# State cleared by VectorE and a new written-out order for the early tasks of a retention and feed-forward kernel

## The chip, the cores and the metric

The kernel runs on one core of a Trainium2 chip. The metric is the device time in microseconds (us), the median of several runs. The profile is of one execution of the same program.

## The reference

The inputs q, k and v have 4 batches, 8 heads, 768 steps and a head dimension of 64. First comes a retention layer: per head a state decays by gamma and takes in an outer product at each step, and the output is the query times the state. Then, on the 512 columns of all heads together, come a layer norm and a feed-forward block with a residual.

```python
for t in range(S):
    state = gamma[None, :, None, None] * state + np.einsum('bhd,bhe->bhde', k[:, :, t], v[:, :, t])
    y[:, :, t] = scale * np.einsum('bhd,bhde->bhe', q[:, :, t], state)
# x: y as (B, S, H * D)
xn = (x - mu) / np.sqrt(var + 1e-06) * g_ln
ch = np.maximum(xn @ w_ch1, 0.0) @ w_ch2
return x + ch
```

The weights are 512 x 2048 and 2048 x 512.

## The kernel before

**Tiles.** The 4 x 768 rows are 24 tiles of 128 rows. Tiles 0 to 3 are the first chunk of each batch, tiles 4 to 8 the chunks 1 to 5 of batch 0, and so on. Within a tile the retention is computed as masked attention; between the chunks of a batch it goes through the state (`pb` in the planner, the tile `state` on the chip, two buffers).

**Loads.** GpSimd issues the loads of q, k and v (one tile each, L430) and of the weights (L438), which arrive converted to bf16. Each weight is loaded in four quarters, here w1_0 to w1_3 and w2_0 to w2_3. Only q and k of tile 0 come another way (L401). From tile 9 on a small copy into `scrap` (L447) makes a load wait until an earlier load has landed.

**The tasks of a tile t** below 8, with the names used further on:

- tk, tq: TensorE transposes k and q into PSUM (L498, L505). ek: ScalarE copies k out (`trk`, L256). eq: VectorE scales q out (`trq`, L510).
- pa: TensorE, scores (L538). am: VectorE masks them into `asb` (L562). py: TensorE, scores times v (L586), and from chunk 1 on the query times `state` (L582).
- bn, xn: VectorE, statistics and the normalised row tile (L601, L613). xc: ScalarE keeps a copy of the row (L619).
- tx: TensorE transposes xn (L672), ex: ScalarE copies it to `xnt` (L256). sq and rs give `rstd` (L694 on ScalarE, L700 on VectorE).
- vg: GpSimd scales v (L633); pd: TensorE adds k times vg to the running sum in PSUM (L645); pb: VectorE writes the diagonal blocks of `state` from it (L659). The other blocks of `state` stay zero, which is why both buffers are cleared once (`c_zero`, L341).
- m1(g, ho): TensorE, group g of rows times four 128-column blocks of the first weight (L719), which starts at block ho. In the first eight groups a group is one tile, so m1(g, 0) needs w1_0, m1(g, 4) needs w1_1, m1(g, 8) w1_2, m1(g, 12) w1_3. re: relu on ScalarE (L732) or VectorE (L734).
- m2: TensorE, the second weight (L757), which needs all of w2; VectorE adds the residual (L767) and ScalarE sends the result off (L774).

From tile 8 on the transposes of q and k are made by DMA (L520), issued from SyncE.

**What sets the order.** The tasks are numbered as they are added. The list `ORDER`, written out by hand, gives the sequence in which they are emitted: a number modulo 10000 is the task, the ten thousands choose the engine where two are possible, the hundred thousands one of two PSUM banks. Every engine runs its own tasks in that sequence. The class `Plan` goes through the list with a fixed cost for each task and each load and so has a planned start for each. These planned times serve one purpose: `fill` looks at TensorE's planned gaps before `FILL_END` (14 us) and before the first task that takes `pd`, and puts matmuls on a zero tile there (L785) for a share `FILL` of the gap. `w_pad` is the time that the planner adds to the landing of a weight quarter.

Of the kernel before, what the change touches and what calls it, by code (L numbers as in the profile page):

```python
# [14 lines left out]
PE, ACT, DVE, POOL, SP = range(5)  # L15
# [4 lines left out]
              "k3", "q3", "v3", "w1_2", "k4", "q4", "v4", "k5", "q5", "v5", "w1_3", "w2_0",  # L20
              "k6", "q6", "v6", "k7", "q7", "v7", "w2_1", "w2_2", "w2_3"],
    "bufs": {"qsb": 6, "ksb": 5, "vsb": 9, "qk": 8, "tr": 6, "vg": 3, "trq": 3, "trk": 3},
    "load_pad": 600, "w_pad": 1500, "lead": 32, "lead2": 32, "sq_at": 28000, "late_load": 1700, "two": 4, "m2b": ("b0",), "m2all": 16, "inter": 4, "every": 4, "tail": (0, 384, 512), "step": 8, "pace": 8, "ahead": 3,
    "slack": 600, "tr_pad": 4000, "x_pad": 3500, "vg_pad": 2500, "fill": 0.8, "fill_end": 14000,
}

ORDER = [int(x) for x in """
16 17 2 0 3 19 20 23 14 8 15 1 24 5 7 9 25 4 10 6 21 11 26 18 22 146 45 100147 149 148  # L30
27 150 28 151 153 46 162 100163 29 152 154 164 165 30 155 12 166 31 156 167 32 157 158
159 47 168 176 13 524 169 179 214 100177 170 525 33 215 178 171 172 216 180 34 173 181
532 35 526 36 533 182 37 190 527 534 183 193 38 100191 184 535 48 192 185 186 194 187
195 49 540 542 541 196 204 543 528 197 39 207 100205 198 536 529 40 200 42 43 41 206 544
50 217 234 52 51 53 10537 55 208 100224 54 199 201 545 550 209 225 548 551 210 227 44
226 251 202 549 552 228 218 56 211 546 553 547 222 275 212 219 538 229 235 220 100241
554 539 530 10555 221 213 242 244 531 243 230 231 556 560 57 174 557 258 561 245 261 236
232 233 558 100237 562 238 246 259 247 10559 260 566 563 564 567 262 252 570 203 248 249
254 565 188 255 568 60 250 569 263 100722 160 61 58 59 268 62 287 253 298 63 723 716 724
301 66 264 67 64 717 65 725 269 718 161 571 175 189 719 265 726 266 720 576 100271 270  # L40
276 307 267 578 272 579 577 239 728 273 68 69 278 277 72 729 730 731 318 73 279 70 299
71 280 580 572 732 281 300 282 74 322 284 223 286 734 735 75 288 581 283 285 736 302 303
290 289 573 737 291 738 574 319 584 292 740 741 293 320 294 296 742 308 304 240 585 78
575 743 582 744 295 297 310 333 79 76 309 77 339 586 305 583 311 80 746 587 334 747 312
335 313 314 274 316 323 81 256 315 748 84 350 749 351 588 592 317 325 85 82 83 379 750
589 257 324 354 326 727 602 86 752 87 753 327 328 329 603 593 590 754 755 594 591 330 90
331 340 352 332 342 756 341 343 721 380 598 321 599 595 91 758 336 759 344 760 761 596
733 88 345 89 355 762 346 368 348 353 600 92 757 745 739 337 597 347 93 764 96 349 97 94
381 601 95 765 98 338 357 604 356 766 606 386 99 605 382 607 767 358 306 359 383 614 612
768 360 384 615 361 613 363 770 397 102 771 103 100 362 772 398 365 364 763 369 101 104  # L50
371 370 773 403 610 372 608 774 611 373 776 616 609 399 366 105 374 387 108 109 617 375
618 414 367 377 106 107 777 620 418 751 376 378 389 619 110 388 778 390 779 622 415 391
385 404 780 392 393 621 623 630 782 395 111 114 429 115 631 394 112 400 456 113 433 626
116 624 117 396 406 120 121 416 405 430 783 627 625 407 784 431 408 628 419 409 634 785
410 629 632 411 412 457 118 119 122 413 421 635 786 445 633 420 123 788 126 458 422 127
789 646 124 423 424 790 425 427 647 401 125 426 428 791 642 638 434 436 792 435 794 795
796 639 643 465 769 437 438 640 417 439 440 442 128 797 459 641 129 441 446 443 476 132
644 798 432 402 133 645 636 130 448 447 648 131 134 138 637 460 650 449 450 649 800 651
461 451 452 801 802 477 454 803 444 775 480 462 453 466 478 455 135 491 804 136 137 468
492 467 806 139 495 807 469 470 140 493 808 471 141 809 472 142 474 473 475 652 653 654  # L60
481 483 482 484 810 655 656 658 143 510 479 485 144 787 506 805 657 799 145 659 660 661
486 662 507 496 487 489 664 663 488 508 490 666 498 497 665 499 667 668 670 669 500 671
501 502 672 673 504 511 812 674 503 505 676 513 512 675 514 678 463 677 680 515 679 682
813 681 814 683 516 494 811 509 517 781 519 464 518 520 815 100830 831 816 521 832 818
819 200824 820 825 684 817 793 685 826 690 688 691 827 689 694 696 833 695 522 686 697
687 708 709 821 698 699 692 693 523 822 848 700 828 834 702 100842 701 703 706 707 704
200836 714 837 705 715 712 838 849 843 713 710 711 850 844 845 839 846 851 840 100854
852 855 856 823 847 841 835 829 853 857 860 861 858 862 863 864 859 865
""".split()]


# [90 lines left out]
def kernel(  # L162
# [16 lines left out]
    nc = tc.nc  # L179
# [158 lines left out]

    def c_zero(eng):
        for x in state:  # L340
            nc.gpsimd.memset(x, 0.0)  # L341

    a = plan.add
    small = a(DVE, 1200, -100, c_small)
# [11 lines left out]
    qscd = a(ACT, 700, -91, c_qsc, [args, table])  # L356
    maskd = a(DVE, 1230, -50, c_mask, [vscd, tri])
    gchd = a(ACT, 900, 100, c_gch, [small, qscd, vscd], at=9000)
    zerod = a(POOL, 500, 0, c_zero, at=9000)
    exps = [gchd, qscd, vscd]  # L360

    def c_gb(eng):
# [101 lines left out]
    for g in range(NG):  # L464
        for ho in range(HO):
            unit["1", g, ho] = u
            u += GROUPS[g] / 4
            every = CFG["every"] if GROUPS[g] == 1 else 8 if 12 <= G0[g] < 16 and GROUPS[g] == 2 else 4
# [239 lines left out]
    for g in range(NG):  # L708
        n = GROUPS[g]
        hb, h0 = buf_of[g]  # L710
        two = GMAX // n
# [109 lines left out]
```

## Time and profile before

| | |
|---|---|
| time, median of 3 runs | 214.54 us (214.35 to 215.2) |
| span of the profiled execution | 213.4 us |
| TensorE busy | 203.9 us (96%) |
| VectorE, ScalarE, GpSimd busy | 119.8, 86.3, 96.4 us |
| granted TensorE clock | 1.000 |
| moved by DMA | 26.85 MB |
| GpSimd's two memsets of `state` | 1.11 us, from 12.40 us |
| filler matmuls (L785) | 24, from 1.18 to about 12 us |

The busy times overlap; an engine's share says how full it is and not what it costs. The chain that ended last consists of TensorE for 87%, DMA for 4%, GpSimd for 4% and ScalarE for 2%. In the lines of the profile a group shows its start or its busy time, the engine, the line of the code and what it writes and reads; brackets hold the idle time ahead of it and what ended that.

### The profile page before, as it was taken

The numbers are of one execution on the slowest core, as the hardware profiler recorded it, in microseconds if no ns is written. First come the engines' busy times: TensorE is split into PE (matmuls) and PEld (weight loads), VectorE is DVE, ScalarE is ACT, GpSimd is POOL, SyncE is SP. The second block draws the span as 40 slices with busy tenths as digits, with TensorE's granted clock in tenths as the row PEclk, the third lists the DMA queues.
The fourth block names the chain that finished last, engine by engine and source line by source line (L and its number), as shares of the span: only waits on it lengthen the run. The fifth ranks groups of instructions, "written<-read, shape, count | busy, mean of one in ns | idle before, by whom it ended". The sixth has DMA issues, their size and how long they took to land.

```text
span 213.4 us, 4941 instructions
## 1 busy us (share of the span) xinstructions
PE 203.9 (96%) x2005; PEld 130.6 (61%) x2027; DVE 119.8 (56%) x260; ACT 86.3 (40%) x175; POOL 96.4 (45%) x151
## 2 busy tenths in 40 slices
PE   7977999999999999999999999999999999999992
PEld 3457989985667666666676676574454444444452
DVE  4876666863665874663775777578676510030041
ACT  5465677660421333332352442351376601544200
POOL 8997797249577464667845947430000000000000
PEclk9999999999999999999999999999999999999999
DMA  9999999999999999999999999939440250000035
GB/s 128 177 179 180 164 195 177 207 133 121 128 98 100 111 125 158 177 269 154 128 112 198 96 184 102 159 76 147 100 151 1 84 164 3 0 0 0 0 145 202
DMA packets 108890, 26.85 MB, mean 126 GB/s; under 512 B 101569, under 2 KB 105921, under 8 KB 108866
## 3 DMA queue, kind: packets, MB, share of 16 engines
q0 software_dynamic: 77024, 13.37, 81.2%
q1 hardware_dynamic: 27186, 6.59, 21.0%
q10 hardware_dynamic: 4656, 6.56, 8.8%
q8 instruction: 16, 0.26, 0.5%
q14 instruction: 8, 0.07, 0.1%
HBM read 27.30 MB, written 6.29 MB: 157 GB/s over the span
## 4 chain that ended last, share of the span: by engine, by line
PE 87%; DMA 4%; POOL 4%; ACT 2%; issue 1%; DVE 0%; POOLq 0%
PE b L757 39%; PE mm L719 38%; DMA k<-in_k_dram 4%; PE pa L538 2%; PE pd L645 2%; PE b L572 2%; PE b L548 2%; POOL v L430 1%; POOL k L430 1%; POOL qsb L430 1%; POOL w L438 1%; PE b L498 1%; ACT L694 1%; PE b L672 1%; ACT h L732 1%
## 5 line engine op out<-in xcount | busy, mean ns | idle before, releaser
L719 PE MATMUL mm<-xnt,w 128*128 128x128 bf16 (+2 forms) x896 | 95.2, 257 | 1.0 <-ACT xnt L256 0.9
L757 PE MATMUL b<-w,h 128*128 128x512 bf16 (+2 forms) x379 | 88.4, 370 | 1.2 <-issue 0.2
L732 ACT ACTIVATE h<-mm 128x512 bf16<-128x512 f32 x93 | 55.0, 598 | 83.6 <-PE mm L719 80.5
L719 PEld LDWEIGHTS <-w 128*128 128x128 bf16 x896 | 66.1, 98 | 21.4 <-issue 1.1
L757 PEld LDWEIGHTS <-h 128*128 128x128 bf16 x400 | 37.0, 98 | 37.7
L562 DVE TENSOR_TENSOR asb<-pa,mask 128x1024 bf16<-128x1024 f32 x24 | 29.4, 1224 | 19.6 <-PE pa L538 19.2
L767 DVE SCALAR_TENSOR_TENSOR osb<-b,rstd,x_all 128x512 f32<-128x512 f32 (+2 forms) x25 | 18.0, 727 | 27.3 <-PE b L757 27.0
L601 DVE BATCH_NORM_STATS2 bns<-b 128x6 f32<-128x256 f32 (+1 forms) x40 | 17.8, 478 | 17.4 <-PE b L572 11.0
L619 ACT CAST x_all<-b 128x256 bf16<-128x256 f32 (+1 forms) x40 | 16.2, 417 | 22.6 <-DVE xn L613 20.1
L613 DVE SCALAR_TENSOR_TENSOR xn<-b,mv,gb 128x256 bf16<-128x256 f32 (+1 forms) x40 | 20.1, 533 | 0.8
L633 POOL TENSOR_TENSOR vg<-vsb,vsc 128x512 bf16<-128x512 bf16 x16 | 16.6, 1044 | 5.6 <-PE pd L645 5.3
L430 POOL DMA_DIRECT2D vsb<-in_v_dram x20 | 18.1, 906 | 1.7 <-issue 1.6
L659 DVE TENSOR_TENSOR state<-pd,gch 64x256 bf16<-64x256 f32 x40 | 16.6, 414 | 4.1 <-PE pd L645 3.2
L430 POOL DMA_DIRECT2D qk<-in_k_dram x16 | 14.3, 892 | 2.2 <-issue 2.2
L430 POOL DMA_DIRECT2D qk<-in_q_dram x16 | 14.2, 886 | 1.0 <-issue 1.0
L447 POOL COPY scrap<-vsb 1x1 bf16<-1x1 bf16 x15 | 2.6, 176 | 19.2 <-DMA vsb<-in_v_dram 19.2
L447 POOL COPY scrap<-qk 1x1 bf16<-1x1 bf16 x30 | 5.3, 176 | 13.0 <-DMA qk<-in_k_dram 11.1
L700 DVE RECIPROCAL rstd<-rstd 128x1 f32<-128x1 f32 (+2 forms) x14 | 2.0, 157 | 13.4 <-ACT rstd L694 13.4
L785 PE MATMUL pd<-zeros 128*128 128x512 bf16 (+1 forms) x24 | 6.6, 420 | 1.3 <-DVE zeros L291 1.2
L572 PEld LDWEIGHTS <-asb 128*128 128x128 bf16 x128 | 5.8, 98 | 2.4
L438 POOL DMA_DIRECT2D w<-in_moe_w_ch_dram x8 | 6.3, 787 | 2.1 <-DMA w<-in_moe_w_ch_dram 2.0
L430 POOL DMA_DIRECT2D qsb<-in_q_dram x7 | 6.4, 909 | 1.8 <-DMA k<-in_k_dram 1.3
(68 smaller groups left out, 127.7 us busy)
## 6 DMA issues: line engine op xcount, KB each, us to landing
out_dram<-osb ACTq DMA_DIRECT2D x23, 256.0 KB, 3.4
w<-in_moe_w_ch_dram POOLq DMA_DIRECT2D x8, 512.0 KB, 10.3
vsb<-in_v_dram POOLq DMA_DIRECT2D x20, 128.0 KB, 5.5
qk<-in_k_dram POOLq DMA_DIRECT2D x16, 128.0 KB, 5.0
qk<-in_q_dram POOLq DMA_DIRECT2D x16, 128.0 KB, 5.2
qsb<-in_q_dram POOLq DMA_DIRECT2D x7, 128.0 KB, 8.9
v<-in_v_dram POOLq DMA_DIRECT2D x4, 128.0 KB, 6.7
ksb<-in_k_dram POOLq DMA_DIRECT2D x4, 128.0 KB, 9.4
```

Of the source, the lines that this page charges most:

```text
L430: nc.gpsimd.dma_start(out=tile_of(kind, j), in_=src)
L562: nc.vector.tensor_tensor(out=take("asb", t, [P, NPAIR, 2, P], BF16).rearrange("p i a t -> p a i t"), in0=held["pa", t], in1=mask.rearrang ...
L572: nc.tensor.matmul(half_y[h % 2][:, h // 2 * D:(h // 2 + 1) * D], lhsT=held["asb", t][:, h // 2, h % 2, :], rhs=tile_of("v", t)[:, h, :], ...
L601: nc.vector.bn_stats(out=bns[:, t, i, :], in_=x)
L613: nc.vector.scalar_tensor_tensor(out=dst, in0=src, scalar=mv[:, t, 0:1], in1=g, op0=ALU.subtract, op1=ALU.mult)
L619: nc.scalar.copy(out=dst, in_=src)
L633: e.tensor_tensor(out=take("vg", j, [P, H, D], BF16), in0=tile_of("v", j), in1=vsc[:, cc, :].unsqueeze(2).to_broadcast([P, H, D]), op=ALU. ...
L659: nc.vector.tensor_tensor(out=held["pb", n][o, :, o], in0=held["pd", b][o, :, o], in1=gch[o, cc, :].unsqueeze(2).to_broadcast([D, NPAIR, D ...
L719: nc.tensor.matmul(p[:, j, :], lhsT=w1[:, ko, (ho + j) * P:(ho + j + 1) * P], rhs=held["xnt", hb][:, h0:h0 + n, ko, :], start=(ko == 0), s ...
L732: nc.scalar.activation(out=dst, in_=src, func=AF.Relu)
L757: nc.tensor.matmul(held[key][:, 0:w], lhsT=held["h1", hb][:, ho, i * P:(i + 1) * P], rhs=w2[:, ho, cols], start=(ho == 0), stop=(ho == HO ...
L767: nc.vector.scalar_tensor_tensor(out=take("osb", key, [P, w], FP32), in0=held[key][:, 0:w], scalar=rstd[:, t:t + 1], in1=x_all[:, t, cols] ...
```

## The change

VectorE clears the two buffers of the state, in the stretch where the constants are made, instead of GpSimd between the loads. The list `ORDER` has a new first part, searched with landing times of the loads that were measured; the first 291 of its 866 entries are rearranged, and the rest is as it was. `w_pad` goes from 1500 to 550. No arithmetic changes.

```diff
-    "load_pad": 600, "w_pad": 1500, "lead": 32, "lead2": 32, "sq_at": 28000, "late_load": 1700, "two": 4, "m2b": ("b0",), "m2all": 16, "inter": 4, "every": 4, "tail": (0, 384, 512), "step": 8, "pace": 8, "ahead": 3,
+    "load_pad": 600, "w_pad": 550, "lead": 32, "lead2": 32, "sq_at": 28000, "late_load": 1700, "two": 4, "m2b": ("b0",), "m2all": 16, "inter": 4, "every": 4, "tail": (0, 384, 512), "step": 8, "pace": 8, "ahead": 3,
...
-16 17 2 0 3 19 20 23 14 8 15 1 24 5 7 9 25 4 10 6 21 11 26 18 22 146 45 100147 149 148
-27 150 28 151 153 46 162 100163 29 152 154 164 165 30 155 12 166 31 156 167 32 157 158
+16 17 2 0 3 19 20 23 14 8 15 1 24 5 7 9 25 4 10 6 13 21 11 26 18 45 22 27 44 28 146 46
+100147 149 148 150 151 29 30 31 32 47 162 152 165 214 33 100163 153 164 154 155 166 156
...
     def c_zero(eng):
         for x in state:
-            nc.gpsimd.memset(x, 0.0)
+            nc.vector.memset(x, 0.0)
...
-    zerod = a(POOL, 500, 0, c_zero, at=9000)
+    zerod = a(DVE, 480, -94, c_zero)
```

Read by engine, the list's new part is as follows. TensorE, tasks 11 to 64 (the first ten and all from the 65th on are the same):

```text
before: tk2 m1(0,0) tq2 pd0 tx1 pa2 m1(1,0) m1(0,4) py2 tk3 m1(1,4) tq3 tx2 pa3 m1(2,0)
        m1(2,4) py3 tk4 m1(0,8) tq4 m1(1,8) tx3 m1(2,8) pa4 | tk5 m1(3,4) tq5 m1(3,0) py4
        m1(3,8) pa5 pd4 m1(2,12) m1(1,12) pd5 tx4 tk6 m1(3,12) m1(0,12) tq6 py5 m1(4,0)
        m1(4,8) tk7 pa6 m1(4,4) tx5 m1(4,12) tq7 py6 m1(5,4) m1(5,0) pa7 pd6
after:  tk2 tq2 m1(0,0) pa2 pd0 tx1 m1(0,4) py2 m1(1,4) tk3 m1(1,0) tq3 tx2 pa3 m1(2,0)
        m1(1,8) py3 tk4 m1(2,8) tq4 m1(0,8) tx3 m1(2,4) pa4 | tk5 pd4 tq5 m1(3,0) m1(3,4)
        py4 pd5 m1(3,12) m1(3,8) pa5 tx4 m1(2,12) m1(0,12) py5 m1(1,12) tk6 m1(4,0) tq6
        m1(4,4) tx5 m1(4,8) pa6 tk7 tq7 m1(4,12) m1(5,4) py6 m1(5,0) pd6 pa7
```

GpSimd, where a name is a load and `clear` the memsets:

```text
before: v0 k1 q1 v1 w1_0 k2 q2 w1_1 v2 k3 q3 v3 w1_2 clear vg0 k4 q4 v4 k5 q5 v5 w1_3 w2_0
        k6 q6 k7 q7 v6 w2_1 vg4 vg5 w2_3 w2_2 k8 v8 q8 v7 vg6 ...
after:  v0 k1 q1 v1 w1_0 k2 v7 q2 w1_1 v2 k3 q3 v3 w1_2 vg0 k4 q4 v4 k5 q5 v5 w1_3 vg4 w2_0
        k6 vg5 q6 q7 w2_3 w2_1 k7 v6 w2_2 v8 k8 vg6 q8 ...
```

ScalarE has the first square root, with the load of its table, right after ex of tile 0; before, the first one stood after ek of tile 5 (the table load at 29.83 us). VectorE gets the clearing ahead of the cast of q0, and five relus of this part in place of three.

## The prediction

> **What bounds the kernel now.** I read the busy slices of the page first, then the list of what TensorE waited for, then the timelines of TensorE and of GpSimd, and last the single DMA issues with their times to landing.
>
> ```profile
> PE   7977999999999999999999999999999999999992
> DMA  9999999999999999999999999939440250000035
> ```
>
> From the fifth slice (about 21 us) on, TensorE is 90% busy or more until the last slice. The DMA engines are busy from the second slice on. By GpSimd's timeline the loads are a continuous stream until about 48 us, and from there each waits for an earlier one. So the end is set by TensorE's amount of work plus whatever TensorE loses, and what it loses lies early. The list of TensorE's waits sizes the loss:
>
> ```profile
> PE pd L785 <- DVE zeros L291: 1.2, 1, 1.2
> PE mm L719 <- ACT xnt L256: 0.9, 2, 0.5
> PE pd L645 <- POOL vg L633: 0.8, 1, 0.8
> PE b L498 <- DMA k<-in_k_dram: 0.6, 1, 0.6
> PE pa L538 <- DVE trq L510: 0.3, 1, 0.3
> ```
>
> Without the first (the start) these are 2.6 us, all between 12 and 22 us. That is the most that a better order can bring by closing these waits. In TensorE's timeline the wait for the keys of tile 3 and, later, the stretch around the keys of tile 7 look like this:
>
> ```profile
> 18.68 0.40 PE L498 MATMUL b<-idn,k 128*128 128x128 bf16 x4 [0.65 <-DMA k<-in_k_dram]
> ...
> 38.66 0.39 PE L498 MATMUL b<-idn,ksb 128*128 128x128 bf16 x4
> 38.98 0.40 PE L538 MATMUL pa<-trq,trk 64*128 64x128 bf16 x8
> ...
> 44.22 0.40 PE L645 MATMUL pd<-vg,ksb 128*128 128x128 bf16 x4
> 44.46 1.06 PE L719 MATMUL mm<-xnt,w 128*128 128x128 bf16 x16
> ```
>
> The transposes at 38.66 are those of k7 and waited for nothing. At 44.46 the 65th task of TensorE's order begins, the first from which its old and new orders are the same, so 44.46 is my mark. GpSimd's timeline gives the loads:
>
> ```profile
> 12.40 1.11 POOL L341 MEMSET state<- 128x512 bf16 x2
> 13.36 1.16 POOL L633 TENSOR_TENSOR vg<-v,vsc 128x512 bf16<-128x512 bf16 x1
> ...
> 19.26 0.89 POOL L430 DMA_DIRECT2D qsb<-in_q_dram  x1 [1.28 <-DMA k<-in_k_dram]
> ...
> 22.52 0.74 POOL L438 DMA_DIRECT2D w<-in_moe_w_ch_dram  x1 [0.74 <-DMA w<-in_moe_w_ch_dram]
> ...
> 25.59 0.88 POOL L430 DMA_DIRECT2D ksb<-in_k_dram  x1
> ```
>
> The eighteenth load (q5) waits for the tenth (k3), the twenty-first for the thirteenth: eight loads are in flight, and GpSimd issues the next when the oldest has landed. And one issue of k (k7's):
>
> ```profile
> ksb<-in_k_dram POOLq DMA_DIRECT2D x1, 128.0 KB, 9.9
> ```
>
> Issue plus time to landing gives each landing: k7 25.6 + 9.9 = 35.5, in the same way k2 12.2, q2 12.9, w1_1 15.5, v2 16.5, k3 18.7, w1_2 22.3, k4 23.3, v4 25.2, v5 28.0, w1_3 30.0, w2_0 32.5, k6 33.4, q7 36.0, v6 36.8, w2_1 39.4, w2_3 41.9, w2_2 44.4, k8 45.3, v7 47.8. They land in the order of issue. From w2_1 to w2_2 a weight quarter takes 2.5 us. From v1 (9.0) to v7 (47.8) eight weight quarters and 21 tiles land in 38.8 us. With the quarters' own steps, 19.5 us together, a tile takes (38.8 - 19.5) / 21 = 0.92 us.
>
> **What the Trainium skill says.** "DMA: Bandwidth & Descriptors", Queues, rings and completion order: on each DMA engine descriptors are consumed in ring order. The landings above agree, so a load moved forward pushes back all that it overtakes. "TensorE: Matmul & The Clock Gate", The mechanism: matmuls start and end strictly in order. TensorE's timeline of before does follow the written order, so a transpose whose data is late stops all behind it. The same page, What's actually happening: the clock halves after an idle window of about 3.4 us. The waits of before, 0.8 us at most from 2 us on, kept the granted clock at 1.00, and no wait forecast below reaches 3.4 us. "ScalarE: Activation LUTs", What ACT_TABLE_LOAD costs: about 1283 ns for the load, and a drain. The trace has 1.28 us at 29.83 us.
>
> **The change, part by part.**
> *Clearing the state.* The two GpSimd memsets (1.11 us at 12.4) go. On VectorE each clears 128x512 bf16; `zeros`, of the same size, took 0.27 us there, so 0.54 us. Upper bound 1.1 us, GpSimd's own time. The new place is just ahead of the cast of q0, before which VectorE sat idle 1.50 us (to 4.87, for q0's DMA). It costs nothing. The saved GpSimd time is spent at once: v7's issue (0.87 us) comes ahead of the same point. vg of tile 0 starts at about 13.2 instead of 13.36.
>
> *v7 as the seventh load instead of the thirty-third.* Every load from q2 to v6 gets one tile more ahead of it: +0.92 us. q2 13.8, w1_1 16.4, v2 17.4, k3 19.6, w1_2 23.2, k4 24.2, v4 26.1, v5 28.9, w1_3 30.9, w2_0 33.4, k6 34.3. Only after v7's old place are the sums equal again.
>
> *TensorE to pa of tile 4, its 34th task.* Both orders hold the same tasks up to there. The new one puts tq2 ahead of the first m1 (the L719 products). tk2 ends at 12.5, q2 lands at 13.8: 1.3 us are lost, where before the m1 had filled them. If the planner sees this gap (it ends before FILL_END, 14 us), it puts filler matmuls there: a filler in place of a wait, with the same effect. The smaller `w_pad` can do no more than that either, since it enters only the planner's due times. From there with the pitches of the trace (m1 0.89, pa 0.33, the others 0.22 to 0.23): tq2 to 14.1, m1 15.0, pa2, pd0, tx1 to 15.8, then m1 on w1_1 from 16.4 to 17.3, py2 after v2 (17.4) to 17.6, m1 to 18.5, tk3 on k3 at 19.6. Before, tk3 began at 18.68. Then m1(1,0), tq3, tx2 and pa3 to about 21.9, m1(2,0) 22.0 to 22.9 (21.62 before), m1 on w1_2 from 23.2 to 24.1, and eight tasks of known length (3.9 us) to the end of pa4 at 28.0. Before: 27.4. So +0.6 us, with 0.79 us for vg gone and more lost to landings. The early square root on ScalarE (1.28 + 0.3 us from 12.0) puts trk of tile 2 at 14.1 instead of 13.3, still ahead of pa2 at 15.0: nothing. Two relus more than before (0.69 us each) go to VectorE, which is busy 3.3 to 4.1 us in each 5 us here: nothing, beside TensorE's waits for loads.
>
> *vg4 and vg5 moved between the loads on GpSimd.* They wait for v4 (26.1) and v5 (28.9), and behind them in the queue stand w2_0, k6 and q6. w2_0 is issued at about 27.2 instead of 22.5. The transfers under way last until w1_3 at 30.9. The quickest w load of the trace took 6.3 us from issue to landing, so 27.2 + 6.3 = 33.5 against 33.4 by the stream: hidden, narrowly.
>
> *k7 behind w2_3 and w2_1.* Before, q6, k7, q7 followed k6. Now q6, q7, w2_3, w2_1, k7. From k6 at 34.3: 0.9 + 0.9 + 2.5 + 2.5 + 0.9 gives k7 at 42.0. On TensorE the 57th task is tk7 in the new order. From pa4 at 28.0 the tasks up to it are ten m1 (8.9 us), four of tk and tq (0.9), two tx and two pd (0.9), py4 and py5 (0.9), pa5 and pa6 (0.7), 12.3 us together. TensorE arrives there at 40.3 and waits 1.7 us. All m1 products behind it wait as well. From there to the mark stand tk7, tq7, three m1, py6, pd6, pa7: 0.22 + 0.22 + 2.68 + 0.46 + 0.22 + 0.33 = 4.1 us. 42.0 + 4.1 = 46.1, plus about 0.1 for the semaphore: 46.2. Before: 44.46. **+1.7 us.** The early 0.6 us is not added, it is swallowed in this wait.
>
> *After the mark.* The order is the old one. vg6 waits for v6 (42.9), so q8 behind it goes out at 44.0 and lands at about 49 instead of 47.0. Its transpose takes 5.2 us, to 54.3, and its use on VectorE was at 55.8 before, now 1.7 us later: hidden. w2_2 lands at 45.4, and its first use is at 46.47 + 1.7. TensorE's idle time after 50 us, from the windows, is under 1.2 us, so nearly nothing of the delay can be won back.
>
> Sum: 214.54 + 1.7 = **216.2 us**.
>
> **Rivals.** *A, no change, 214.6 us.* For it k7 would have to land by 40.3. Speaking for it: the stream's rate swings (w1_3 came in 2.0 us), and the mark may be reached later in other ways before too. Against it: two quarters would have to come 0.9 us quicker each than all three w2 quarters of the trace that can be timed. *B, faster, 213.2 us.* Half of the 2.6 us of waits closes, and the rate of the stream rises as GpSimd's memsets go. For it: the new order does take away the vg wait of 0.79 us and part of those for xnt. Against: the DMA rate is set by its engines, full in every slice. *C, slower still, 217.3 us.* The loads blocked behind vg4 and vg5 leave the DMA engines empty for about 1 us, or the first square root holds up ScalarE's relu. For: the narrow 0.1 us above.
>
> **How the numbers follow.** The forecast 0.65, A 0.13, B 0.12, C 0.10. Half a per cent is 1.07 us, so the forecast (+1.7) and C are both slower by more, except a small part of the forecast that comes out under it: slower 0.74, same 0.14, faster 0.12. Range: low end 214.4, to take in A; high end 217.3, C. B is left out.
>
> **What would show it.** In the changed profile: memsets of `state` on VectorE near 3.5 to 4.9 us with no new wait; a wait or filler ahead of tq2 near 13.5; tk3 at 19.6 with a longer DMA wait than 0.65; TensorE's list headed by a wait of about 1.7 us at L498 for the DMA of k, near 42; the first m1 after pd6 at about 46.2. Wrong if k7 lands by 40.5, if TensorE reaches tk7 after k7, or if the mark is later and the end isn't.

## The result and the profile after

The changed kernel takes 221.03 us (median of 4 runs, 220.42 to 222.32) against 214.87 us of the kernel before in the same comparison. The ratio is 1.028, with a 95% interval from 1.0204 to 1.0357. Here and below a median holds all runs, while a ratio leaves out those that are over 1.5% longer than the fastest of the same kernel. The forecast was 216.2 us with a range up to 217.3: slower, as said, but by more than three times as much.

The page of the changed kernel, its span and two rows of busy slices (40 equal slices, tenths; PEclk is the clock that TensorE was granted):

```profile
span 218.9 us, 4937 instructions
...
PE   6978999499999999999999999999999999999992
...
PEclk9999999969999999999999999999999999999999
```

The eighth slice (38 to 44 us) was full before and is half empty now, and in the ninth the clock is down for the only time. TensorE's list of waits (total, times, longest) has a new head:

```profile
PE b L498 <- DMA ksb<-in_k_dram: 3.2, 1, 3.2
PE b L505 <- DMA qsb<-in_q_dram: 1.6, 2, 1.2
PE pd L785 <- DVE zeros L291: 1.2, 1, 1.2
PE mm L719 <- DMA w<-in_moe_w_ch_dram: 0.8, 2, 0.5
```

The 0.8 us for vg and the 0.9 us for xnt are gone from it, replaced by waits for loads. TensorE's timeline around the wait, up to the first common task at 49.68:

```profile
40.23 0.40 PE L538 MATMUL pa<-trq,trk 64*128 64x128 bf16 x8
43.82 0.40 PE L498 MATMUL b<-idn,ksb 128*128 128x128 bf16 x4 [3.19 <-DMA ksb<-in_k_dram]
44.05 0.39 PE L505 MATMUL b<-idn,qsb 128*128 128x128 bf16 x4
44.27 3.10 PE L719 MATMUL mm<-xnt,w 128*128 128x128 bf16 x32
47.16 0.64 PE L582 MATMUL b<-state,trq 128*128 128x128 bf16 x4
...
49.35 0.40 PE L538 MATMUL pa<-trq,trk 64*128 64x128 bf16 x8
49.68 1.07 PE L719 MATMUL mm<-xnt,w 128*128 128x128 bf16 x16
```

This is the wait at tk7 that was forecast, but it ends at 43.8 and not at 42.0. And what follows is slow: 32 m1 matmuls took 1.95 us before and take 3.10 here, py6 0.64 in place of 0.39. The windows say why (the columns are the stretch, its length, busy time of the five engines with counts, then the granted clock, the DMA share and GB/s):

```profile
44.00:46.00 2.00, 2.00 (x30) 2.00 (x28) 0.42 (x1) 0.30 (x1) 1.23 (x2) 0.71 1.87 174
46.00:48.00 2.00, 2.00 (x25) 2.00 (x24) 0.00 (x0) 1.37 (x3) 0.70 (x1) 0.50 1.03 69
48.00:50.00 2.00, 2.00 (x39) 1.79 (x37) 1.67 (x5) 0.60 (x2) 1.03 (x2) 0.94 0.82 58
```

TensorE is fully busy in all three, but at 0.71, 0.50 and 0.94 of its clock. A busy share alone would hide this.

So 5.2 us of the span's 5.5 are lost by the mark (49.68 against 44.46). They fall into 1.7 us that were forecast, 1.8 us by which k7 came later than worked out (43.8 against 42.0), and 1.7 us by which the stretch from tk7 to the mark took longer (49.68 - 43.82 = 5.9 against 4.1).

### The profile page after: what moved, and what is told of

The parts are those of the page before. It is cut to its first block, busy times and chain, and to the rows that moved or that the text cites. A ratio compares the mean times of both kernels' runs of the same rounds, so it can differ in the third digit from the quotient of the medians.

```text
span 218.9 us, 4937 instructions
## 1 busy us (share of the span) xinstructions
PE 205.5 (94%) x2005; PEld 131.9 (60%) x2027; DVE 121.3 (55%) x264; ACT 85.3 (39%) x173; POOL 95.8 (44%) x149
## 4 chain that ended last, share of the span: by engine, by line
PE 78%; DMA 12%; POOL 7%; issue 1%; DVE 1%; DVEq 0%; POOLq 0%
PE b L757 35%; PE mm L719 33%; DMA ksb<-in_k_dram 5%; DMA w<-in_moe_w_ch_dram 5%; PE pa L538 2%; DMA out_dram<-osb 2%; POOL qsb L430 2%; PE pd L645 2%; PE b L572 2%; POOL v L430 2%; PE b L548 2%; POOL w L438 1%; POOL k L430 1%; DVE osb L767 1%; POOL vg L633 0%
## 5 line engine op out<-in xcount | busy, mean ns | idle before, releaser
L719 PE MATMUL mm<-xnt,w 128*128 128x128 bf16 (+2 forms) x896 | 96.8, 260 | 0.8 <-DMA w<-in_moe_w_ch_dram 0.8
L757 PE MATMUL b<-w,h 128*128 128x512 bf16 (+2 forms) x379 | 88.4, 370 | 1.2 <-issue 0.2
L732 ACT ACTIVATE h<-mm 128x512 bf16<-128x512 f32 x91 | 53.8, 598 | 87.0 <-PE mm L719 86.8
L719 PEld LDWEIGHTS <-w 128*128 128x128 bf16 x896 | 67.1, 99 | 21.5 <-DMA w<-in_moe_w_ch_dram 1.2
L757 PEld LDWEIGHTS <-h 128*128 128x128 bf16 x400 | 37.0, 98 | 37.7
L527 DVE TENSOR_TENSOR trq<-tr,qsc 128x512 bf16<-128x512 bf16 x16 | 7.0, 439 | 0.1
```

The lines of the kernel that those rows point to most:

```text
L719: nc.tensor.matmul(p[:, j, :], lhsT=w1[:, ko, (ho + j) * P:(ho + j + 1) * P], rhs=held["xnt", hb][:, h0:h0 + n, ko, :], start=(ko == 0), s ...
L732: nc.scalar.activation(out=dst, in_=src, func=AF.Relu)
L757: nc.tensor.matmul(held[key][:, 0:w], lhsT=held["h1", hb][:, ho, i * P:(i + 1) * P], rhs=w2[:, ho, cols], start=(ho == 0), stop=(ho == HO ...
```

## The experiments

Where the list `ORDER` is edited, some line numbers move by one (L499 for L498). In the short diffs a name is a load of GpSimd's queue. All ratios are to the kernel before, run beside them.

**k7 and v6 moved back.**

```diff
-... k6 vg5 q6 q7 w2_3 w2_1 k7 v6 w2_2 ...
+... k6 vg5 q6 q7 k7 v6 w2_3 w2_1 w2_2 ...
```

> The changed kernel with two loads moved: k7 and v6 are issued right behind q7, ahead of w2_3 and w2_1. Theory (all of the loss is the wait for k7 and the slow clock behind it): k7 lands at about 37 us, TensorE reaches tk7 at 40.5 without a wait, the first common task begins at 44.8 instead of 49.7, the granted clock stays 1.00, and the time is 215.3 us. Rival (the loss comes from several places, the early v7, the blocked GpSimd queue, the early square root): at least 2 us of it stay, 217 us or more.

Measured: 215.89 us, ratio 1.0018 (0.9997 to 1.0039). The wait at tk7 is gone from TensorE's list. Two loads moved over two weight quarters take away nearly the whole loss. The rival falls: with k7 early, the early v7, the blocked queue and the early square root leave 0.4 us together, by the interval 0.8 us at most. (What the blocked queue costs while k7 is late is another matter, and has its own run below.) In the profiled execution the early loads came late and the mark was 45.92 instead of 44.8, which will be taken up below.

**k7 alone made late, in the kernel before.**

```diff
-... k6 q6 k7 q7 v6 w2_1 vg4 vg5 w2_3 w2_2 ...
+... k6 q6 q7 v6 w2_1 vg4 vg5 w2_3 k7 w2_2 ...
```

> The kernel before with one load moved: k7 is issued behind w2_3 instead of behind q6. Theory: k7 lands at about 41.9 us, TensorE, which reaches tk7 at 38.7, waits 3.2 us, the clock drops behind it as in the changed kernel, and the time is about 219.5 us: this one move makes nearly all of the loss. If the clock doesn't drop: 217.8 us. Rival (the move alone is harmless because TensorE makes up for it later): 215 us.

Measured: 220.43 us, ratio 1.0221 (1.018 to 1.0263). TensorE's timeline in this kernel:

```profile
42.37 0.40 PE L499 MATMUL b<-idn,ksb 128*128 128x128 bf16 x4 [3.24 <-DMA ksb<-in_k_dram]
42.70 0.40 PE L539 MATMUL pa<-trq,trk 64*128 64x128 bf16 x8
43.03 1.79 PE L720 MATMUL mm<-xnt,w 128*128 128x128 bf16 x16
```

Sixteen matmuls in 1.79 us, for 1.06 at full clock; from 44 to 46 us the granted clock was 0.50. The mark came at 49.80, 5.3 us late. One load in the wrong place does it by itself, and nothing later in the kernel made up for it. The drop of the clock comes with it in most runs only: averaged over a whole run, the granted clock was 0.989, 0.983 and 0.992 in three of the four and 1.000 in the fourth, which still took 219.59 us. So most of this loss is there without the drop.

**TensorE kept busy during the wait.**

```diff
+            if t is plan.tasks[258]:
+                p = take("mm", "fill", [P, 4 * P], FP32)
+                for _ in range(14):
+                    nc.tensor.matmul(p, lhsT=zeros[:, 0:P], rhs=zeros, start=True, stop=True)
             t["emit"](t["eng"])
```

> The changed kernel with 14 matmuls on the zero tile (3.0 us) put ahead of tk7, so that TensorE waits for k7 without being idle; they compute nothing that is used. Theory (the idle time let the clock drop, which cost 1.7 us between 44.3 and 49 us): granted clock 1.00, the first common task at about 48.0 instead of 49.7, time 219.3 us. Rival (the slow matmuls there have another cause, such as the weights or the relus being late): no change from 221.0 us.

Measured: 218.16 us, ratio 1.0119 (1.0082 to 1.0156), below the changed kernel's interval. TensorE's timeline:

```profile
40.75 3.19 PE L793 MATMUL mm<-zeros 128*128 128x512 bf16 x14
43.78 0.39 PE L498 MATMUL b<-idn,ksb 128*128 128x128 bf16 x4
44.00 0.39 PE L505 MATMUL b<-idn,qsb 128*128 128x128 bf16 x4
44.23 1.95 PE L719 MATMUL mm<-xnt,w 128*128 128x128 bf16 x32
...
48.01 1.07 PE L719 MATMUL mm<-xnt,w 128*128 128x128 bf16 x16
```

tk7 begins when it did (43.78), the m1 behind it are back to 1.95 us, and the mark is at 48.01 as expected, 1.67 us earlier. Averaged over a whole run, the granted clock was 1.000 in three of the four runs and 0.991 in the fourth; in the changed kernel it was 0.984 to 0.992 in all four. Work that computes nothing made the kernel faster, because the idle time costs a second time afterwards.

The medians differ by 2.9 us, the spans of the two profiled executions by 2.8 (218.9 and 216.1), 1.1 us more than the mark's shift. These 1.1 us lie behind TensorE. Its last group of matmuls (L757) begins 157.16 us after the mark here, 157.15 in the changed kernel and 157.14 before, so a shift of the mark goes through to the end unchanged. But the last store of a result, 64 KB, took 1.6 us from issue to landing here, 2.6 in the changed kernel and 2.4 before. The fillers' own gain is the 1.7 us at the mark; why the store was quicker, and whether it was in the other runs too, is open.

**Fewer fillers.** The same edit with `range(5)`.

> The changed kernel with 5 matmuls on the zero tile (1.1 us) ahead of tk7 in place of 14, so that about 2.1 us of the wait for k7 are idle. Theory (the clock drops only after an idle time of about 3 us): granted clock 1.00 behind the wait, time as with 14 of them, 218.2 us. Rival (any idle time of 2 us is enough): slow matmuls from 44 to 48 us and about 221 us.

Measured: 219.54 us, ratio 1.0167 (1.0119 to 1.0215), four runs from 218.1 to 221.9. The profiled one, which took 218.1 us, had 1.9 us of idle time at tk7 and a clock of 1.00 behind it. The other three are longer, and their granted clock, averaged over the run, was 0.992, 0.991 and 0.991. In the changed kernel's profiled execution the one drop of the clock makes an average of 0.992, so each of these three has a loss of the size of one such drop. No timeline shows where it fell. But with 14 fillers, in a kernel otherwise the same, only one run of four has it, so tk7 is the likely place. That speaks for the rival, that about 2 us of idle time can be enough, and against the theory of about 3 us.

**vg4 and vg5 moved out of the way.**

```diff
-... w1_3 vg4 w2_0 k6 vg5 q6 q7 w2_3 w2_1 k7 v6 ...
+... w1_3 w2_0 k6 q6 vg4 q7 w2_3 w2_1 vg5 k7 v6 ...
```

> The changed kernel with vg4 moved behind q6 and vg5 behind w2_1 in GpSimd's queue, so that neither holds back an issue; k7 stays behind both weight quarters. Theory (the prediction's stream of landings was right, and the 1.8 us by which k7 came later than 42.0 are DMA engines left empty behind the blocked issues): k7 lands at 42.0 to 42.3, TensorE waits 1.4 to 1.7 us, the clock stays at 1.00, time 217.5 us. If the clock drops at this shorter wait too: 219.2 us. Rival (k7 is late because the transfers themselves are slower there): k7 lands at 43.5 or later as before, 221 us.

Measured: 217.12 us, ratio 1.0101 (1.0056 to 1.0146). From issue to landing, w1_3 and k7:

```profile
w<-in_moe_w_ch_dram POOLq DMA_DIRECT2D x1, 512.0 KB, 9.4
...
ksb<-in_k_dram POOLq DMA_DIRECT2D x1, 128.0 KB, 10.9
```

With their issues at 22.01 and 31.55, w1_3 landed at 31.4 and k7 at 42.45: 11.0 us for three quarters and four tiles, where the prediction had 11.1 (30.9 to 42.0). In the changed kernel it was 30.75 to 43.76, 13.0 us. TensorE's wait at tk7, and the mark:

```profile
42.52 0.40 PE L499 MATMUL b<-idn,ksb 128*128 128x128 bf16 x4 [1.19 <-DMA ksb<-in_k_dram]
...
46.76 1.07 PE L720 MATMUL mm<-xnt,w 128*128 128x128 bf16 x16
```

The clock stayed at 1.00 in this execution (in two of the seven runs its average is 0.989 and 0.992). The mark is 2.9 us earlier than in the changed kernel: k7 landed 1.3 us earlier, and from tk7 to the mark it took 4.2 us in place of 5.9. The wait is 2.0 us shorter and not 1.3, because TensorE came to tk7 0.7 us later here. The forecast as a ratio, 216.2 / 214.54 = 1.0077, lies in this kernel's interval: it had priced the change without the blocked issues. The windows of the changed kernel show where its DMA engines fell short:

```profile
29.00:32.00 3.00, 3.00 (x62) 3.00 (x60) 2.28 (x6) 1.77 (x4) 3.00 (x4) 1.00 1.20 184
...
34.00:37.00 3.00, 3.00 (x61) 3.00 (x59) 2.08 (x4) 1.54 (x5) 3.00 (x4) 1.00 1.53 150
```

And the same stretches with vg4 and vg5 out of the way:

```profile
29.00:32.00 3.00, 3.00 (x61) 3.00 (x58) 2.32 (x5) 2.43 (x6) 3.00 (x5) 1.00 1.33 201
...
34.00:37.00 3.00, 3.00 (x64) 2.90 (x59) 1.88 (x3) 2.24 (x5) 2.51 (x3) 1.00 1.50 199
```

Read the last column: 150 GB/s against 199 from 34 to 37 us, 184 against 201 from 29 to 32. That is (49 + 17) x 3 = 198 KB not moved, about 1.0 us at this rate. The bytes of the load queue agree: at 30.75 us both kernels had moved about the same (4.56 MB in the changed kernel, 4.59 here), at 42.45 us 6.57 against 6.75 MB. So the short rate makes 0.8 to 1.0 us (an estimate from these figures) of the 1.3 us by which k7 landed later in the changed kernel (43.76 against 42.45); the rest was not taken apart. The other 0.7 of the 2.0 us (13.0 against 11.0) is only where the count begins, since w1_3 landed at 30.75 there and at 31.4 here. The cause of the short rate is in GpSimd's timeline of the changed kernel:

```profile
26.01 1.04 POOL L633 TENSOR_TENSOR vg<-vsb,vsc 128x512 bf16<-128x512 bf16 x1 [3.81 <-DMA vsb<-in_v_dram]
27.00 0.80 POOL L438 DMA_DIRECT2D w<-in_moe_w_ch_dram  x1
27.80 0.89 POOL L430 DMA_DIRECT2D ksb<-in_k_dram  x1
28.70 1.06 POOL L633 TENSOR_TENSOR vg<-vsb,vsc 128x512 bf16<-128x512 bf16 x1
29.69 1.82 POOL L430 DMA_DIRECT2D qsb<-in_q_dram  x2
31.49 1.51 POOL L438 DMA_DIRECT2D w<-in_moe_w_ch_dram  x2
```

GpSimd stands still for 3.81 us at vg4, with nothing issued from 22.2 to 27.0, and again for vg5's 1.06 us. When w2_3 is issued at 31.5, four loads are still under way instead of eight.

**Parts of the change alone, in the kernel before.** The clearing on VectorE:

> The kernel before with the clearing of the state alone moved to VectorE. Theory: nothing to be had, although vg of tile 0 starts 1.1 us earlier and TensorE's wait of 0.8 us for it goes: the wait for k3 at tk3 grows by as much (from 0.65 to about 1.4 us), since k3 is issued ahead of the memsets and lands when it did. Time as before within 0.3 us. Rival (the vg wait was worth its length): 0.8 us faster.

Measured: 215.42 us, ratio 0.9989 (0.9963 to 1.0016): nothing. The wait for vg is gone, and a wait of 1.0 us for a load of k stands in its place, in this execution for k2 rather than k3.

v7 as the seventh load:

> The kernel before with v7 alone moved to be the seventh load. Theory (a load moved forward delays all it overtakes by one tile, 0.9 us): k3 and w1_2 land about 0.9 us later, TensorE's waits between 12 and 24 us grow by 0.6 to 0.9 us and the time by as much, 0.3 to 0.4%. Rival (the stream has room): no change.

Measured: 216.75 us, ratio 1.0023 (0.9986 to 1.006). The mark came at 45.39, 0.9 us later than before, as forecast for one tile. But the interval holds 1 too: its price in the whole time isn't settled, and it is no large part.

The clearing on VectorE and k3 ahead of w1_1:

> The kernel before with the clearing on VectorE and k3 issued ahead of w1_1. Theory: with the clearing away, what holds TensorE in the stretch from 14 to 19 us is k3 alone; k3 now lands near 14 and w1_1 near 16.4, about when its first product comes, so tk3 begins near 17.7 instead of 18.7, tq3 then waits for q3 at 19.1, and 0.5 to 0.7 us are gained: ratio 0.997. Rival (another landing takes the place of k3's): no change.

Measured: 215.55 us, ratio 0.9978 (0.9942 to 1.0013), inconclusive. tk3 began at 18.84 and not at 17.7: py2, ahead of it, now waits 0.8 us for v2, which k3 had overtaken.

**The new orders of the engines with the old loads.** First with vg5 behind w2_1:

```diff
-... k2 v7 q2 ... w1_3 vg4 w2_0 k6 vg5 q6 q7 w2_3 w2_1 k7 v6 w2_2 v8 k8 vg6 q8 ...
+... k2 q2 ... w1_3 w2_0 k6 q6 vg4 k7 q7 v6 w2_3 w2_1 vg5 w2_2 v8 k8 vg6 q8 v7 ...
```

> The changed kernel with GpSimd's loads in nearly the order of before (v7 last, k7 and v6 ahead of the weight quarters, vg4 and vg5 behind q6 and w2_1); TensorE's, VectorE's and ScalarE's new orders stay. Theory (all of the loss sits in GpSimd's queue): the time of before within 0.5 us. Rival (the new order of TensorE, with tq2 ahead of the first m1, or the early square root has a share): 0.5 to 1 us slower than before.

Measured: 217.29 us, ratio 1.0079 (1.0057 to 1.0101). This was of the experiment's own making, since w2_1's issue held vg5 back and pd5, which the new order has early, waited 1.8 us for it:

```profile
32.15 0.38 PE L646 MATMUL pd<-vg,ksb 128*128 128x128 bf16 x4 [1.78 <-POOL vg L634]
```

Then with vg5 right behind k7:

> As the kernel with nearly the old order of loads (v7 last, k7 and v6 ahead of the weight quarters), but vg5 right behind k7 instead of behind w2_1, so that pd5 doesn't wait for it. Theory (all of the changed kernel's loss sits in GpSimd's queue, and the 1.8 us of the run before this one were vg5's wait alone): the first common task of TensorE begins at 44.2 to 44.5, the time is that of the kernel before within 0.5 us. Rival (the new order of TensorE or the early square root costs something by itself): 1 us slower or more, with waits at other places.

Measured: 214.84 us, ratio 0.9974 (0.9957 to 0.9991). The mark is at 44.47, and TensorE's list holds only these waits of 0.7 us and more:

```profile
PE pd L786 <- DVE zeros L292: 1.2, 1, 1.2
PE mm L720 <- DMA w<-in_moe_w_ch_dram: 0.9, 2, 0.5
PE b L499 <- DMA k<-in_k_dram: 0.7, 1, 0.7
```

The clearing, the smaller `w_pad`, the early square root, the relus on VectorE and TensorE's new order cost nothing together. With the loads in nearly their old order this version is 0.26% faster than the kernel before, and the only one of all whose interval lies below 1. Where these 0.26% lie its profile doesn't show: mark and span (213.4 us) are those of the kernel before.

## Why the prediction was half right

**Held.** *Direction and place*: slower, through tk7's wait for k7 behind w2_3 and w2_1. Putting that right brings the time back (1.0018), and doing it alone to the kernel before makes the loss (1.0221). *TensorE's arrival*: forecast for 40.3, measured 40.6. *tq2*: k, q and the first m1 went as worked out, with a wait of 1.19 us at tq2, which began at 13.96; no filler took its place. *The clearing*: VectorE did it from 3.37 us in 0.55 us, the cast of q0 came no later (4.84 against 4.87), and by itself it changes nothing. *The early square root*: 1.28 us of table load at 12.06, and no wait of TensorE behind it. The drain that the Trainium skill ("ScalarE: Activation LUTs", What ACT_TABLE_LOAD costs) has beside the load doesn't show: the next activation begins 0.02 us after it. *The order of landings*: in the changed kernel too the loads landed in the order of issue, from k2 (12.3) and v7 (13.3) to k7 (43.8) and v6 (44.6). In "DMA: Bandwidth & Descriptors", Queues, rings and completion order, the sentence on ring order stands in a paragraph on the queues of SyncE and ScalarE, so for GpSimd's loads the order rests on these landings. *vg4's block*: w2_0 issued at 27.0, forecast 27.2. *After the mark*: nothing was won back, as the 157.15 us to TensorE's last matmuls show (157.14 before).

**Mis-sized.** *"k7 at 42.0"*: it landed at 43.8. The step that failed is the one on vg4 and vg5, "hidden, narrowly". It compared one load, w2_0, with the end of the transfers under way (33.5 against 33.4; it landed at 33.9) and stopped there. The loads behind it were just as short of lead: w2_3 was issued at 31.5 and landed at 39.2 instead of 38.6, w2_1 at 42.9 instead of 41.1. With the block taken away the stream took 11.0 us for what had been put at 11.1, and k7 landed at 42.45. This is rival C's mechanism, and it came on top of the forecast instead of in place of it.

*"No wait forecast below reaches 3.4 us"*: true of the 1.7 us forecast, and that was the weakness. The wait became 3.2 us, and the half clock behind it cost 1.7 us at the mark (the filler run). No case of the prediction held a term for the clock. The Trainium skill ("TensorE: Matmul & The Clock Gate", What's actually happening) gives an idle window of about 3.4 us; here an idle time measured at 3.19 us, and 3.24 in the second kernel, already led to the drop, and in the runs with five fillers some 2 us seem to have been enough.

*tk3 at 19.6* was wrong by 0.9 us: k3 landed at 18.3, since a load's place in the stream is good for about 1 us only. It didn't matter, because q3 and w1_2 (20.3 and 23.1) came when they were due.

**Sum.** 1.7 + 1.8 + 1.7 = 5.2 us at the mark, 5.5 us in the span, with the rest in the stores at the end. The measured 1.028 is 6.0 us, with an interval that goes down to 4.4 us.

**Left open.** Why the last store took 1.0 us longer in one execution than in another, the part of k7's delay that the short rate doesn't make (0.3 to 0.5 us of 1.3) and the 0.45 us by which it came after 42.0 even without the block, the price of v7's early place, and the length of idle time at which the clock falls. That the search used landing times measured with the old order of loads, and so took k7's late place for free, would fit what is seen; it was not tried.

## What to carry to other kernels

When loads share one full stream, a landing time belongs to the order it was measured in: move a load over others and add up the bytes again, before the consumers' order is written. A compute instruction that waits for a load holds back every issue behind it in its queue; compare each of those issues with the moment at which the transfers already issued run out, not the first of them alone. And a wait forecast near the length at which the clock falls needs a second term for the slow work behind it.

## What was not expected of the hardware

The clock also fell where no single idle time was near 3 us. In the profiled execution of the kernel with k7 and v6 moved back, two waits that lie close together, 1.08 us at tk2 and 1.26 us at tq2, were enough:

```profile
13.73 0.40 PE L499 MATMUL b<-idn,k 128*128 128x128 bf16 x4 [1.08 <-DMA k<-in_k_dram]
15.38 0.61 PE L506 MATMUL b<-idn,qsb 128*128 128x128 bf16 x4 [1.26 <-DMA qsb<-in_q_dram]
15.79 1.91 PE L720 MATMUL mm<-xnt,w 128*128 128x128 bf16 x16
```

The 16 m1 matmuls took 1.91 us in place of 1.06, and the granted clock was 0.76 from 14 to 16 us and 0.50 from 16 to 18. An average of 0.76 over 2 us is about 1 us at half clock (an estimate), so the drop came near 15.0, before the second wait was over. In the changed kernel's profiled execution the same place had one wait, 1.19 us, and the clock stayed at 1.00. With vg4 and vg5 out of the way it had two, 0.78 and 1.28 us, and the clock stayed at 1.00 as well. So the longest idle time doesn't settle whether the clock falls. That the drop hangs on how much TensorE did over some microseconds would fit; no run here tests it. How early the loads happen to land plays a part: in five kernels with the same early loads, tk2 began between 12.37 and 13.73 us.
